# Two AV runs of two head pairs, even fill and late sums in an attention-plus-MoE kernel

## The chip, the cores and the metric

The kernel runs on one core of one Trainium2 chip. The metric is device time in microseconds (us) of one execution. Smaller is better.

## The reference

What is computed, in short. B = 8 batches, H = 8 heads, S = 576 tokens, D = 64:

```python
scores = q @ k.T / sqrt(D)
cum = cumsum(log(clip(f, 1e-4, 1)))              # along the tokens
scores = where(causal, -1e9, scores + cum[:, None] - cum[None, :])
attn = softmax(scores)
x = attn @ v                                     # heads side by side: [4608, 512]
h = x @ w_in                                     # [4608, 2048]
g = 0.5 * h * (1 + erf(h / sqrt(2)))
out = g @ w_out                                  # [4608, 512]
```

The decay is folded into the values: V and a column of ones are multiplied by a weight per key (L253), and the sum of that column divides the result (L318).

## The kernel before, in words

The work goes batch by batch. Each batch has two stages on TensorE (PE): its attention, then GEMM1 (L370), which multiplies the transposed attention output xT of the batch by w_in, 16 blocks of four matmuls, each followed by a gelu on ScalarE (ACT). GEMM2 of a batch isn't a stage of its own: it is the fill of the attention one batch later. The tails of 64 tokens of all batches are put together and go through both GEMMs at the end.

The order on every engine is the order in which the code is written (a manual schedule); nothing moves an instruction. An engine takes its instructions in that order. GEMM2 is a generator, and `take(fill, n)` (L521) writes its next n steps at that point. The lists FILL and FILL_2 (L617, L618) say how many steps follow each score tile.

**Scores.** A pair i holds two heads, on 64 rows of the array each. `scores(b, i, t)` (L270) writes four tiles per pair; a tile takes both heads. Its matmuls use 64 rows, two side by side. ACT takes the exp of each tile (L299) and GpSimd (POOL) clears the entries above the diagonal (L301). The pool `s` has two buffers of two PSUM banks, so a score tile needs the exp of the tile two before it. I write S(i,t) and exp(i,t).

**AV.** `attend` (L313) makes 15 matmuls of 128 rows for one head into a buffer `o`; `normalize` (L318) takes the reciprocal (L333) and multiplies (L334) on VectorE (DVE). Pool `o` has two buffers of one bank, and pool `m` as well. `av(i)` (L627) does both heads of a pair, after S(i+1,1). AV of the last pair comes after all scores.

**Transposes of x.** `x_dma` (L358) lets a DMA on SP's queue do it; `to_xT` (L346) does it on PE, with a copy on DVE. In the batches from 3 on, pairs 0 to 2 go by DMA and pair 3 by PE. In batch 2, pair 2 goes by PE too.

**Fill.** `gemm2_rows(c, plan)` (L446) takes four blocks (ts) of 128 tokens, 16 steps of K = 128 each. A step "n" is one matmul of 128 rows into the first bank. A step "r" is two row-tiled matmuls of 64 rows, one into each of two banks, so an r block needs two banks and a sum at its end: a copy of the second bank (L474), an add of the first (L476), the store (L480). A plan gives each block its pool and its steps (PLAN at L431). Batch 2 has its own fill (L516): half of two blocks of batch 0 (L485, whole matmuls in `m`), two blocks of batch 0 (PLAN_0), then four of batch 1 (PLAN_1).

Batches 0 and 1 have their own functions, which the change leaves alone. A buffer of a pool is given out again when the last reader of what it held is done; of two, the one first free.

Of the kernel before, what the change touches and what calls it, by code (L numbers as in the profile page):

```python
# [1 line left out]

# [6 lines left out]
FP32 = mybir.dt.float32  # L9
BF16 = mybir.dt.bfloat16  # L10
Act = mybir.ActivationFunctionType
Alu = mybir.AluOpType
PSUM = bass.MemoryType.PSUM

P = 128
S = 576
D = 64
H = 8
HP = 4
NBLK = 5  # L20
# [32 lines left out]
def kernel(  # L53
# [10 lines left out]
    nc = tc.nc  # L64
# [5 lines left out]
    n_ff = d_ff // P  # L70
# [17 lines left out]
    s_psum = ctx.enter_context(tc.tile_pool(name="s_psum", bufs=2, space=PSUM))  # L88
    o_psum = ctx.enter_context(tc.tile_pool(name="o_psum", bufs=2, space=PSUM))
    m_psum = ctx.enter_context(tc.tile_pool(name="m_psum", bufs=2, space=PSUM))  # L90
# [46 lines left out]
    for t, op, fill in (  # L137
# [7 lines left out]
            fill=fill,  # L145
# [164 lines left out]

    o_of, x_of, xT_of = {}, {}, {}

    def attend(b, i, h, ms):  # L313
        if (b, i, h) not in o_of:
            o_of[b, i, h] = o_psum.tile([P, NBLK, D + 1], FP32, tag="o", name="o")
        o = o_of[b, i, h]
        for m in ms:
            for n in range(m + 1):  # L318
                t, c = where(n, m)
                nc.tensor.matmul(  # L320
                    o[:, m, :],
                    e_of[b, i, t][:, h, c : c + P],
                    vw_of[b][:, 2 * i + h, n, :],
                    start=(n == 0),
                    stop=(n == m),
                )

    def normalize(b, i, h):
        if (b, i) not in x_of:
            x_of[b, i] = x_pool.tile([P, NBLK, 2, D], BF16, tag="x", name="x")  # L330
        o = o_of[b, i, h]
        r = x_pool.tile([P, NBLK], FP32, tag="r", name="r")
        nc.vector.reciprocal(r, o[:, :, D])  # L333
        nc.vector.tensor_tensor(  # L334
            x_of[b, i][:, :, h, :],
            o[:, :, 0:D],
            r.unsqueeze(2).to_broadcast([P, NBLK, D]),
            Alu.mult,
        )
# [6 lines left out]
    def to_xT(b, i, copy, pool=m_psum, tag="m", ps=None):  # L346
        if ps is None:
            shape = [P, 2, 1024] if pool is s_psum else [P, XC]
            ps = pool.tile(shape, BF16, tag=tag, name="ps_x")
            if pool is s_psum:  # L350
                ps = ps[:, 0, 0:XC]
        for m in range(NBLK):
            nc.tensor.transpose(  # L353
                ps[:, m * P : (m + 1) * P], x_of[b, i][:, m, :, :], ident_bf
            )
        copy(xT(b)[:, i, :], ps)  # L356

    def x_dma(b, i):  # L358
        nc.sync.dma_start_transpose(
            xT(b)[:, i, :].rearrange("d (m p) -> d m p", p=P),  # L360
            x_of[b, i].rearrange("p m h d -> p (m h d)"),
        )
# [31 lines left out]
    def gemm2(c):  # L394
# [34 lines left out]


    PLAN = [  # L431
        (0, "o", 16 * "r"),
        (1, "m", 6 * "r" + "n" + 8 * "r" + "n"),
        (2, "m", 9 * "r" + "n" + 6 * "r"),
        (3, "s", 7 * "r" + 9 * "n"),
    ]

    PLAN_0 = [(2, "o", 16 * "r"), (3, "m", 14 * "r" + 2 * "n")]
    PLAN_1 = [
        (0, "m", 14 * "r" + 2 * "n"),  # L440
        (1, "m", 14 * "r" + 2 * "n"),
        (2, "m", 14 * "r" + 2 * "n"),
        (3, "s", 8 * "r" + 8 * "n"),
    ]

    def gemm2_rows(c, plan):  # L446

        for ts, held, steps in plan:
            if held == "s":
                both = s_psum.tile([P, 2, d_model], FP32, tag="s", name="ps2")
                banks = [both[:, 0], both[:, 1]]
            else:
                pool = {"o": o_psum, "m": m_psum}[held]
                banks = [
                    pool.tile([P, d_model], FP32, tag=held, name="ps2")
                    for _ in range(2)
                ]  # L460
            ot = o_pool.tile([P, d_model], FP32, tag="ot", name="ot")
            for kt, step in enumerate(steps):
                last = kt == steps.rindex("r")
                for r in range(2 if step == "r" else 1):
                    rows = slice(r * D, (r + 1) * D) if step == "r" else slice(0, P)
                    nc.tensor.matmul(  # L466
                        banks[r],
                        g_of[c][kt][rows, ts * P : (ts + 1) * P],
                        w_out_sb[rows, kt, :],
                        start=kt == (steps.index("r") if r else 0),  # L470
                        stop=last if r else kt == n_ff - 1,
                    )
                if kt == n_ff - 1 if held == "s" else last:
                    nc.vector.tensor_copy(ot, banks[1])  # L474
                if kt == n_ff - 1:
                    nc.vector.tensor_tensor(ot, ot, banks[0], Alu.add)  # L476
                    store(c, ts, ot)
                yield

    def store(c, ts, ot):  # L480
        nc.sync.dma_start(out[c * S + ts * P : c * S + (ts + 1) * P, :], ot)
# [39 lines left out]
    def take(gen, n):  # L521
        for _ in range(n):
            if next(gen, "end") == "end":
                return
# [89 lines left out]

    FILL = [[7, 6, 3, 3], [1, 3, 3, 2], [1, 3, 3, 3], [1, 3, 3, 3], [8]]  # L617
    FILL_2 = [[8, 8, 8, 8], [8, 8, 4, 4], [4, 4, 4, 4], [4, 4, 4, 4], [8]]  # L618
    FILL_1 = [[0, 0, 0, 0], [0, 0, 0, 0], [2, 2, 2, 2], [2, 2, 2, 2]]

    def attention(b):


        fill = gemm2_third() if b == 2 else gemm2_rows(b - 1, PLAN)
        counts = FILL_2 if b == 2 else FILL

        def av(i):  # L627
            for h in range(2):
                attend(b, i, h, (0, 1, 2, 3, 4))
                normalize(b, i, h)  # L630

        for i in range(HP):
            for t in range(4):
                scores(b, i, t)
                take(fill, counts[i][t])
                if i and t == 1:
                    av(i - 1)
                    if i < HP - 1 or b > 2:
                        x_dma(b, i - 1)
                if t == 1 and i == 0:  # L640
                    load_v(b + 1)
                if b > 2 and t == 0 and i < 2:
                    transpose_dma(b + 1, 4 * i, 4 * i + 4)
                if b == 2 and t == 1 and i == 1:
                    transpose_dma(3, 0, 4)
                    transpose_dma(3, 4, 8)
        take(fill, counts[HP][0])
        if b == 2:
            to_xT(b, HP - 2, nc.vector.tensor_copy, s_psum, "s")
        av(HP - 1)  # L650
        take(fill, 6)
        to_xT(b, HP - 1, nc.vector.tensor_copy, o_psum, "o")
        x_tail(b)
        take(fill, 999)
# [43 lines left out]
    for b in range(B):  # L698
# [8 lines left out]
        for ffb in range(0 if b > 1 else 4, n_ff):  # L707
# [11 lines left out]
            elif b + 1 < B:  # L719
                first, gap = (5, 3) if b == 1 else (0, 4)  # L720
                at, late = divmod(ffb - first, gap)
# [40 lines left out]
```

The softmax here doesn't subtract the row's maximum and nothing guards it: scores larger than these inputs give would overflow.

## Time and profile before

| what | us |
|---|---|
| median of 3 runs (345.62 to 345.96) | 345.62 |
| span of the profiled execution (first to last instruction) | 343.4 |
| PE busy | 328.6 |
| ACT busy | 212.3 |
| DVE busy | 187.0 |
| POOL busy | 124.2 |
| attention of batch 2, to GEMM1 | 33.0 |
| attention of each batch from 3 on, to GEMM1 | 21.8 |
| GEMM1 of each of these batches | 13.9 |

The page gives the span of the profiled execution and no other time of it. The span leaves out what lies before the first instruction and after the last one, some 2.2 us against the median of the runs. Busy times overlap: the engines work side by side, and the shares don't add up to the span. A line of the timeline gives the start and the length in us, the engine, the line of the code, the operation, what it writes and reads, the rows and columns of the array, the shape, and how many instructions are put together. A matmul's length holds its way through the array: the next one starts before it ends, so the cost of one is read from start to start. In brackets stands the time for which the engine was idle, and what ended it.

### The profile page before, as it was taken

The page shows a single profiled execution, that of the slowest core. Times are in us where ns is not written, and L with a number is a line of the kernel's source. Part 1 is how long each engine was busy: PE and PEld are TensorE (multiplying, and loading weights), DVE is VectorE, ACT ScalarE, POOL GpSimd, SP SyncE. Part 2 cuts the span into 40 slices and gives each one's busy share as a digit, 9 for nine tenths or more (in the row PEclk, how much of TensorE's full clock was granted, in tenths as well). Part 3 has the DMA queues.
Part 4 walks back from the last instruction along what each step waited for, and adds up shares of the span by engine and source line. Part 5 has one row for each costly group of instructions (what it writes and reads, how often), then busy time and mean ns, then how long its engine had stood idle before and what let it go on. Part 6 is the DMA issues. An engine that isn't in the chain of part 4 may idle for free.

```text
span 343.4 us, 7895 instructions
## 1 busy us (share of the span) xinstructions
PE 328.6 (96%) x3182; PEld 174.7 (51%) x3227; DVE 187.0 (54%) x424; ACT 212.3 (62%) x296; POOL 124.2 (36%) x256
## 2 busy tenths in 40 slices
PE   7799999999999999999999999999999999999995
PEld 3574555445554456545654565446544654444443
DVE  5660355933467935796479646974597542020011
ACT  5986786773644787368746874687468755504600
POOL 8390672228328034543445243714261430000000
PEclk9999999999999999999999999999999999999999
DMA  8999999989993999578945896499900230011013
GB/s 117 178 176 194 201 166 153 170 158 148 237 184 102 139 192 188 82 101 165 211 121 73 141 212 139 71 160 198 169 31 2 65 88 31 2 61 61 0 38 87
DMA packets 99924, 43.03 MB, mean 125 GB/s; under 512 B 78704, under 2 KB 95344, under 8 KB 99888
## 3 DMA queue, kind: packets, MB, share of 16 engines
q1 hardware_dynamic: 82592, 28.37, 41.4%
q0 software_dynamic: 16896, 13.63, 27.2%
q8 instruction: 25, 0.41, 0.5%
q10 hardware_dynamic: 400, 0.52, 0.4%
q14 instruction: 11, 0.09, 0.1%
HBM read 36.85 MB, written 9.44 MB: 135 GB/s over the span
## 4 chain that ended last, share of the span: by engine, by line
PE 89%; issue 2%; POOL 2%; DVE 2%; ACT 2%; DMA 2%; POOLq 0%; ACTq 0%; DVEq 0%
PE ps L375 36%; PE ps L466 25%; PE o L320 9%; PE ps L408 8%; PE s L289 7%; PE ps L501 2%; ACT e L299 2%; DMA k<-in_k_dram 2%; PE ps_x L353 1%; DVE x L334 1%; POOL q L107 1%; PE ps_f L206 1%; POOL k L107 1%; DVE r L333 0%; DVE xT L356 0%
## 5 line engine op out<-in xcount | busy, mean ns | idle before, releaser
L392 ACT ACTIVATE g<-ps 128x512 bf16<-128x512 f32 x144 | 85.3, 597 | 81.1 <-PE ps L375 81.1
L299 ACT ACTIVATE e<-s 128x896 bf16<-128x896 f32 (+2 forms) x128 | 101.2, 836 | 28.5 <-PE s L289 26.8
L375 PE MATMUL ps<-xT,w_in_sb 128*128 128x512 bf16 x497 | 111.4, 379 | 0.8
L466 PE MATMUL ps<-w_out_sb,g 64*128 64x512 bf16 (+1 forms) x731 | 103.0, 376 | 0.8 <-issue 0.8
L375 PEld LDWEIGHTS <-w_in_sb 128*128 128x128 bf16 x576 | 56.0, 98 | 67.5 <-issue 1.8
L301 POOL TENSOR_SCALAR_AFFINE_SELECT e<-e 128x256 bf16<-128x256 bf16 (+1 forms) x135 | 49.2, 383 | 98.9 <-ACT e L299 98.6
L466 PEld LDWEIGHTS <-g 64*128 64x128 bf16 (+1 forms) x756 | 41.5, 94 | 40.4 <-issue 11.9
L244 DVE COPY qT<-tq 64x288 bf16<-64x288 bf16 x96 | 48.7, 507 | 1.4
L289 PE MATMUL s<-qT,kT 64*128 64x320 bf16 (+4 forms) x384 | 45.8, 276 | 3.6 <-ACT e L299 2.7
L260 POOL TENSOR_TENSOR vw<-v_sb,wT 128x640 bf16<-128x640 f32 x31 | 39.6, 1278 | 23.5 <-DMA v_sb<-in_v_dram 23.3
L320 PE MATMUL o<-vw,e 128*128 128x65 bf16 x960 | 36.8, 194 | 3.5 <-issue 2.4
L474 DVE COPY ot<-ps 128x512 f32<-128x512 f32 x26 | 17.9, 689 | 37.1 <-PE ps L466 35.2
L320 PEld LDWEIGHTS <-e 128*128 128x128 bf16 x960 | 34.8, 98 | 5.3 <-PE ps_x L353 0.3
L244 DVE COPY kT<-tk 64x288 bf16<-64x288 bf16 x96 | 33.0, 343 | 1.6
L334 DVE TENSOR_TENSOR x<-o,r 128x320 bf16<-128x320 f32 x64 | 31.4, 491 | 2.4 <-DVE r L333 0.2
L417 DVE COPY ot<-ps 128x512 f32<-128x512 f32 (+2 forms) x9 | 5.7, 632 | 48.8 <-PE ps L408 31.9
L289 PEld LDWEIGHTS <-kT 64*128 64x128 bf16 x384 | 19.5, 94 | 23.2 <-issue 9.7
L408 PE MATMUL ps<-w_out_sb,g 128*128 128x512 bf16 (+2 forms) x142 | 27.9, 355 | 0.1
L333 DVE RECIPROCAL r<-o 128x5 f32<-128x5 f32 x64 | 12.1, 189 | 27.6 <-PE o L320 27.5
L408 PEld LDWEIGHTS <-g 128*128 128x128 bf16 x144 | 13.5, 98 | 14.5
L476 DVE TENSOR_TENSOR ot<-ot,ps 128x512 f32<-128x512 f32 x26 | 17.9, 687 | 1.5
L365 POOL COPY tails<-xT 128x256 bf16<-128x256 bf16 x8 | 3.2, 399 | 31.3 <-DVE xT L356 31.3
(64 smaller groups left out, 158.1 us busy)
## 6 DMA issues: line engine op xcount, KB each, us to landing
out_dram<-ot SPq DMA_DIRECT2D x32, 256.0 KB, 2.3
v_sb<-in_v_dram SPq DMA_DIRECT2D x24, 256.0 KB, 5.3
q<-in_q_dram POOLq DMA_DIRECT2D x6, 576.0 KB, 6.1
k<-in_k_dram POOLq DMA_DIRECT2D x6, 576.0 KB, 8.2
v_sb<-in_v_dram SPq DMA_DIRECT2D x22, 128.0 KB, 5.1
w_in_sb<-in_moe_w_in_dram POOLq DMA_DIRECT2D x4, 512.0 KB, 6.7
w_out_sb<-in_moe_w_out_dram POOLq DMA_DIRECT2D x4, 512.0 KB, 8.4
q<-in_q_dram POOLq DMA_DIRECT2D x4, 144.0 KB, 4.6
```

The source lines that it names most:

```text
L244: nc.vector.tensor_copy(rows[:, odd], src[odd * D : (odd + 1) * D, 2 * i + h].rearrange("d j p -> d p j"),)
L260: eng.tensor_tensor(vw_of[b][:, hs, :, 0:D], v_sb[:, hs, :, :], w.unsqueeze(3).to_broadcast([P, 2, NBLK, D]), Alu.mult,)
L289: nc.tensor.matmul(to, *ab, start=half < 0, stop=half == 1 or not masked)
L299: nc.scalar.activation(et[:, :, z:c], st[:, :, z:c], Act.Exp, scale=scale)
L301: nc.gpsimd.affine_select(out=et[:, :, c0 + z : c0 + P], in_=et[:, :, c0 + z : c0 + P], compare_op=Alu.is_ge, fill=0.0, base=z, pattern=[[ ...
L320: nc.tensor.matmul(o[:, m, :], e_of[b, i, t][:, h, c : c + P], vw_of[b][:, 2 * i + h, n, :], start=(n == 0), stop=(n == m),)
L334: nc.vector.tensor_tensor(x_of[b, i][:, :, h, :], o[:, :, 0:D], r.unsqueeze(2).to_broadcast([P, NBLK, D]), Alu.mult,)
L375: nc.tensor.matmul(ps, w_in_sb[:, kt, ffb * P : (ffb + 1) * P], src[:, kt, 0:TC], start=(kt == 0), stop=(kt == n_dm - 1),)
L392: nc.scalar.activation(g_of[c][ffb], ps, Act.Gelu)
L408: nc.tensor.matmul(pss[ts][:, c0:c1], g_of[c][kt][:, ts * P : (ts + 1) * P], w_out_sb[:, kt, c0:c1], start=(kt == 0), stop=(kt == n_ff - 1),)
L466: nc.tensor.matmul(banks[r], g_of[c][kt][rows, ts * P : (ts + 1) * P], w_out_sb[rows, kt, :], start=kt == (steps.index("r") if r else 0), ...
L474: nc.vector.tensor_copy(ot, banks[1])
```

## The change

It touches the attention of batches 2 to 7 and its fill.

- AV of pairs 0 and 1 moves to one place, after S(2,1); AV of pairs 2 and 3 comes after all scores. One step of fill stands after each head of pair 0, one and three after those of pair 2, one after the first of pair 3. The DMA transposes of pairs 0 and 1 move along, and that of pair 2 comes after its AV at the end.
- The last two AV pairs of batch 2 write to pool `m`.
- The steps after each score tile change (FILL, FILL_2), and so do the plans: in PLAN, block 0 is in `m` and block 1 in `o`, blocks 0 and 1 have r alone, block 2 has two n after five r, block 3 is n alone.
- The copy of the second bank of block 2 goes to ACT. Its add and store are put off until after the last AV (`put_off`). A block with no r has a copy in place of a sum.
- In batch 2, the PE transpose of pair 2 moves from ahead of the last AV to behind it, and uses pool `o`.

```diff
--- before.py
+++ after.py
@@ -1,4 +1,5 @@
 from contextlib import ExitStack
+from functools import partial
 
 import concourse.bass as bass
 import concourse.tile as tile
@@ -310,9 +311,9 @@
 
     o_of, x_of, xT_of = {}, {}, {}
 
-    def attend(b, i, h, ms):
+    def attend(b, i, h, ms, pool=o_psum, tag="o"):
         if (b, i, h) not in o_of:
-            o_of[b, i, h] = o_psum.tile([P, NBLK, D + 1], FP32, tag="o", name="o")
+            o_of[b, i, h] = pool.tile([P, NBLK, D + 1], FP32, tag=tag, name="o")
         o = o_of[b, i, h]
         for m in ms:
             for n in range(m + 1):
@@ -429,19 +430,20 @@
 
 
     PLAN = [
+        (0, "m", 16 * "r"),
+        (1, "o", 16 * "r"),
+        (2, "m", 5 * "r" + 2 * "n" + 9 * "r"),
+        (3, "s", 16 * "n"),
+    ]
+
+    PLAN_0 = [(2, "o", 16 * "r"), (3, "m", 10 * "r" + 2 * "n" + 4 * "r")]
+    PLAN_1 = [
         (0, "o", 16 * "r"),
-        (1, "m", 6 * "r" + "n" + 8 * "r" + "n"),
-        (2, "m", 9 * "r" + "n" + 6 * "r"),
-        (3, "s", 7 * "r" + 9 * "n"),
+        (1, "m", 16 * "r"),
+        (2, "o", 16 * "r"),
+        (3, "s", 16 * "n"),
     ]
-
-    PLAN_0 = [(2, "o", 16 * "r"), (3, "m", 14 * "r" + 2 * "n")]
-    PLAN_1 = [
-        (0, "m", 14 * "r" + 2 * "n"),
-        (1, "m", 14 * "r" + 2 * "n"),
-        (2, "m", 14 * "r" + 2 * "n"),
-        (3, "s", 8 * "r" + 8 * "n"),
-    ]
+    put_off = []
 
     def gemm2_rows(c, plan):
 
@@ -459,8 +461,9 @@
                     for _ in range(2)
                 ]
             ot = o_pool.tile([P, d_model], FP32, tag="ot", name="ot")
+            late = len(plan) == 4 and ts == 2
             for kt, step in enumerate(steps):
-                last = kt == steps.rindex("r")
+                last = kt == steps.rfind("r")
                 for r in range(2 if step == "r" else 1):
                     rows = slice(r * D, (r + 1) * D) if step == "r" else slice(0, P)
                     nc.tensor.matmul(
@@ -470,12 +473,19 @@
                         start=kt == (steps.index("r") if r else 0),
                         stop=last if r else kt == n_ff - 1,
                     )
-                if kt == n_ff - 1 if held == "s" else last:
-                    nc.vector.tensor_copy(ot, banks[1])
+                if last:
+                    (nc.scalar.copy if late else nc.vector.tensor_copy)(ot, banks[1])
                 if kt == n_ff - 1:
-                    nc.vector.tensor_tensor(ot, ot, banks[0], Alu.add)
-                    store(c, ts, ot)
+                    out_of = partial(rows_out, c, ts, ot, banks[0], "r" in steps)
+                    put_off.append(out_of) if late else out_of()
                 yield
+
+    def rows_out(c, ts, ot, bank, both):
+        if both:
+            nc.vector.tensor_tensor(ot, ot, bank, Alu.add)
+        else:
+            nc.vector.tensor_copy(ot, bank)
+        store(c, ts, ot)
 
     def store(c, ts, ot):
         nc.sync.dma_start(out[c * S + ts * P : c * S + (ts + 1) * P, :], ot)
@@ -614,8 +624,8 @@
 
 
 
-    FILL = [[7, 6, 3, 3], [1, 3, 3, 2], [1, 3, 3, 3], [1, 3, 3, 3], [8]]
-    FILL_2 = [[8, 8, 8, 8], [8, 8, 4, 4], [4, 4, 4, 4], [4, 4, 4, 4], [8]]
+    FILL = [[7, 6, 3, 3], [3, 3, 3, 3], [3, 3, 0, 1], [2, 2, 2, 2]]
+    FILL_2 = [[8, 8, 3, 3], [3, 3, 3, 3], [4, 4, 4, 8], [10, 10, 10, 10]]
     FILL_1 = [[0, 0, 0, 0], [0, 0, 0, 0], [2, 2, 2, 2], [2, 2, 2, 2]]
 
     def attention(b):
@@ -624,19 +634,24 @@
         fill = gemm2_third() if b == 2 else gemm2_rows(b - 1, PLAN)
         counts = FILL_2 if b == 2 else FILL
 
-        def av(i):
-            for h in range(2):
-                attend(b, i, h, (0, 1, 2, 3, 4))
-                normalize(b, i, h)
+        last = (m_psum, "m") if b == 2 else (o_psum, "o")
+
+        def av(i, h, n=0):
+            attend(b, i, h, (0, 1, 2, 3, 4), *(last if i > 1 else ()))
+            normalize(b, i, h)
+            take(fill, n)
 
         for i in range(HP):
             for t in range(4):
                 scores(b, i, t)
                 take(fill, counts[i][t])
-                if i and t == 1:
-                    av(i - 1)
-                    if i < HP - 1 or b > 2:
-                        x_dma(b, i - 1)
+                if (i, t) == (2, 1):
+                    av(0, 0, 1)
+                    av(0, 1, 1)
+                    x_dma(b, 0)
+                    av(1, 0)
+                    av(1, 1)
+                    x_dma(b, 1)
                 if t == 1 and i == 0:
                     load_v(b + 1)
                 if b > 2 and t == 0 and i < 2:
@@ -644,11 +659,16 @@
                 if b == 2 and t == 1 and i == 1:
                     transpose_dma(3, 0, 4)
                     transpose_dma(3, 4, 8)
-        take(fill, counts[HP][0])
+        av(HP - 2, 0, 1)
+        av(HP - 2, 1, 3)
+        if b > 2:
+            x_dma(b, HP - 2)
+        av(HP - 1, 0, 1)
+        av(HP - 1, 1)
+        put_off.pop()()
         if b == 2:
-            to_xT(b, HP - 2, nc.vector.tensor_copy, s_psum, "s")
-        av(HP - 1)
-        take(fill, 6)
+            to_xT(b, HP - 2, nc.vector.tensor_copy, o_psum, "o")
+        take(fill, 5)
         to_xT(b, HP - 1, nc.vector.tensor_copy, o_psum, "o")
         x_tail(b)
         take(fill, 999)
```

## The prediction

> **What bounds the kernel now.** I read the busy shares first, then the chain of waits, then TensorE's timeline for one batch, then ScalarE's and VectorE's for the same stretch. From the page:
>
> ```profile
> PE 328.6 (96%) x3182; PEld 174.7 (51%) x3227; DVE 187.0 (54%) x424; ACT 212.3 (62%) x296; POOL 124.2 (36%) x256
> PE 89%; issue 2%; POOL 2%; DVE 2%; ACT 2%; DMA 2%; POOLq 0%; ACTq 0%; DVEq 0%
> ```
>
> TensorE (PE) is busy for 96% of the span and carries 89% of the chain that ended last. So a microsecond in which TensorE waits is a microsecond of time, and nothing else matters until it makes TensorE wait. The timeline of TensorE in the attention of batch 4 (start, length, engine, line, count):
>
> ```profile
> 154.77 0.38 PE L375 MATMUL ps<-xT,w_in_sb 128*128 128x512 bf16 x1
> 155.08 0.36 PE L289 MATMUL s<-qT,kT 64*128 64x256 bf16 x4
> 155.28 1.68 PE L466 MATMUL ps<-w_out_sb,g 64*128 64x512 bf16 x14
> ...
> 160.45 0.60 PE L466 MATMUL ps<-w_out_sb,g 64*128 64x512 bf16 x4
> 161.21 1.11 PE L320 MATMUL o<-vw,e 128*128 128x65 bf16 x30 [0.16 <-issue]
> 162.25 0.36 PE L289 MATMUL s<-qT,kT 64*128 64x448 bf16 x2
> 162.45 0.81 PE L466 MATMUL ps<-w_out_sb,g 64*128 64x512 bf16 x6
> 163.10 0.30 PE L289 MATMUL s<-qT,kT 64*128 64x320 bf16 x2
> 163.24 0.59 PE L466 MATMUL ps<-w_out_sb,g 64*128 64x512 bf16 x4
> 163.69 0.37 PE L289 MATMUL s<-qT,kT 64*128 64x256 bf16 x4
> 163.88 0.40 PE L466 MATMUL ps<-w_out_sb,g 64*128 64x512 bf16 x2
> 164.28 0.34 PE L289 MATMUL s<-qT,kT 64*128 64x64 bf16 x4
> ```
>
> Three prices are in it. (1) A step of 512 columns, whole ("n") or as a row-tiled pair ("r"), takes 0.2155 us: seven r from 155.28 to the next scores at 156.79. (2) Mode switches. The last whole matmul of GEMM1 starts at 154.77 and the 64-row scores at 155.08: 0.31, where 0.216 is the matmul, so 0.096 for 128 to 64 rows. From 160.45 to the AV run at 161.21 stand two r and one n (the record of the n is missing): 0.76 - 0.647 leaves 0.11 for 64 to 128. (3) A wait: the tile at 164.28 comes 0.40 after the one r before it instead of 0.2155. That r was all the fill there was, and the tile needs the buffer of the score tile two before it, which ScalarE had not yet read.
>
> Scores cost 0.19, 0.16, 0.19, 0.14 for the four tiles of a pair; an AV run of one head 0.48. Attention takes 21.76 us in each of batches 3 to 7 (155.08 to GEMM1 at 176.85), 33.0 in batch 2 (72.50 to 105.50). ScalarE in the same stretch:
>
> ```profile
> 155.19 0.60 ACT L392 ACTIVATE g<-ps 128x512 bf16<-128x512 f32 x1 [0.27 <-PE ps L375]
> 155.80 1.28 ACT L299 ACT_TABLE_LOAD   x1
> 157.10 4.88 ACT L299 ACTIVATE e<-s 128x896 bf16<-128x896 f32 x6
> 162.72 3.07 ACT L299 ACTIVATE e<-s 128x896 bf16<-128x896 f32 x4 [0.74 <-PE s L289]
> ```
>
> The last gelu of GEMM1 ends at 155.79, which is 0.70 after the attention's first score matmul started. An exp starts 0.47 after its 448-column scores, takes 0.92 (0.81, 0.70 for the narrower tiles) and the next two-tiles-later scores follow 0.05 after its end: scores 162.25, tile two later at 163.69, 1.44 in all. VectorE's normalization of the two heads:
>
> ```profile
> 161.88 0.19 DVE L333 RECIPROCAL r<-o 128x5 f32<-128x5 f32 x1 [1.17 <-PE o L320]
> 162.11 0.49 DVE L334 TENSOR_TENSOR x<-o,r 128x320 bf16<-128x320 f32 x1
> 162.52 0.18 DVE L333 RECIPROCAL r<-o 128x5 f32<-128x5 f32 x1
> 162.74 0.49 DVE L334 TENSOR_TENSOR x<-o,r 128x320 bf16<-128x320 f32 x1
> ```
>
> The first head's last matmul starts at 161.65; its PSUM buffer is free at 162.60, plus 0.05 to reach TensorE: 1.00 in all.
>
> **What the Trainium skill says.** "TensorEngine Tiling (Array Packing)", Key Properties: changing the tiling mode drains TensorE. The trace agrees and prices it at 0.10 to 0.11 us each way. The same page, Gotcha 1 (PSUM Pressure): row tiles write to different banks. The trace's r steps do, and that is why an r block needs two free banks before its first pair. "TensorE: Matmul & The Clock Gate", Part 3 (The mechanism): matmuls start and end strictly in program order. Here the r after a waiting tile never ran ahead of it. So everything behind a waiting matmul waits too.
>
> **The change part by part.** Per batch, for batches 3 to 7.
>
> *Switches.* Before, the order has four passages from 128 to 64 rows (start, and after three AV runs) and four back; the new order has two and two. Two pairs of 0.20: -0.40. The fill n between AV runs is in AV's own mode (0.033 from an AV to an n in the trace), so it adds none. Exchanging 6 r for n costs nothing: both take 0.2155.
>
> *Old waits.* The wait at 164.28 (0.18) and another of 0.18 around 168.4, both behind single-r fills in batch 4's timeline: -0.37. The fills there become 3.
>
> *First block in "m".* Block 0 of the r steps moves from the o buffers, free at that point, to the two m buffers, which GEMM1 used last. The second bank is that of the last gelu. It is free at 0.70 + 0.05 = 0.75; the r wants it at 0.20. Queued behind it is all of TensorE: +0.55. Nothing hides it: S(0,0) is issued, and the next instructions are these very r.
>
> *Two pairs of AV in a row.* Four runs share two o buffers. The third run needs the first's normalization: run start + 0.45 + 1.00 = 1.45, where TensorE arrives at 0.48 + 0.22 + 0.48 + 0.22 = 1.39: +0.06. The fourth needs the second's, whose multiply ends at 2.09, plus 0.05: 2.14; TensorE arrives at 1.93: +0.21. Together +0.27. Entering the run: block 1 now holds o; its last r is five r and two score tiles before it, 1.56 before AV, and the copy needs 0.42 + 0.69, its sum 0.72 more. The first run takes the buffer that the copy frees (1.16), the second, 0.70 later, that of the sum: no wait.
>
> *The tail of scores.* After the AV runs six tiles remain with fills 0, 1, 2, 2, 2, 2. Count from the start of S(2,2). S(3,0) needs exp(2,2): not before 1.43; TensorE arrives at 0.19 + 0.14 + 0.22 = 0.54: wait 0.89. S(3,1): 1.43 + 0.19 + 0.43 = 2.05, exp(2,3) is done at 2.03: none. S(3,2): arrives at 2.64, exp(3,0) runs from 1.92 to 2.84, plus 0.05: 2.89, wait 0.25. S(3,3): arrives at 3.51, exp(3,1) starts 0.81 after the one before and takes 0.81: 3.59, wait 0.07. Together +1.20. ScalarE sat idle during the AV run, and no fill can be done ahead of a waiting tile. AV(2,0) then starts at 4.26.
>
> *Late sums.* The copy of block 2's second bank goes to ScalarE (0.58, from L510's ScalarE copy), behind exp(3,3), about 5.4; its first reader is GEMM1 at 9.9. The add goes behind the last normalization and ends at 8.8. Before that stands the transposing matmul at 8.3, which needs the normalization alone. Cost nothing; cover 1.1 us or more.
>
> *DMAs on SP's queue.* Pairs 0 and 1 are transposed later but 9 us before use. Pair 2's x is normalized at 6.36, issued at 6.4; such transfers landed in 2.6 to 3.9 (median 2.8 in the DMA table): 9.2, at most 10.3. GEMM1 reads it with its third matmul at 9.9 + 0.43 = 10.34. Cost nothing, cover 1.1, none at the slowest. The store of block 1 now precedes the transposes and waits for less than they do; stores and V loads have no reader in this stage. POOL's masks have 0.5 or more to spare.
>
> Sum: -0.40 - 0.37 + 0.55 + 0.27 + 1.20 = +1.25. Adding the new order up from 0 instead (10.36 to the first AV, 13.08 to S(2,2), 9.91 more) gives 22.99, against 21.76: +1.23. Five batches: +6.1.
>
> Batch 2: the old order changes mode at eight places down and eight up (its last block mixes r and n around the transposes), the new at four: -0.80. Old wait before the transpose of pair 3 goes, -0.23. New: AV buffers +0.27; the second transpose waits for the late add, +0.22. Its first r block is in o, as before, and its tail has fills of 8 to 10, over 1.7 us per tile against an exp of 0.92: no tail wait. Sum -0.54; added up from 0, 32.5 against 33.0: -0.5.
>
> In all +6.1 - 0.5 = +5.6 us. The profiled span of 343.4 becomes 349.0; about 2.2 us lie between span and the median of 345.62, unchanged: 351.2.
>
> Bounds: the tail between 0.9 (only the first wait) and 1.4; the gelu wait between 0 (if the allocation differs) and 0.6; AV buffers 0 to 0.5; the direct step from r to AV, which the trace of before lacks, is taken like r to n, 0.11, at most 0.3; never below nothing, since the array must empty. The transfer of pair 2: 0 to 0.6.
>
> **Rivals.** A measurement of this kernel can tell about 0.2%, 0.7 us, from no change.
> - *Pair 2's transfer lands late.* At 4.5 us, what the tq transposes take in the DMA table, it lands at 10.9: 0.58 more, five times: 354.1. Against: the queue is then free, and its like took 2.6.
> - *The gelu wait is covered*, as if the r block began with a free bank: -2.75: 348.5. Against: the order builds r on the buffer of the last gelu.
> - *Only the score tail is covered*: 1.25 - 1.20 = 0.05 a batch, 345.4, no change.
> - *Faster: the mode switches decide.* If neither gelu, AV buffers nor exps hold TensorE, each batch gains 0.77 and batch 2 0.5: 341.3. It decides once the new waits of a batch sum to less than 0.77; for that the tail's first wait would have to vanish, with an exp path of 0.54 where 1.44 is measured.
>
> **How the numbers follow.** My forecast 0.80, late transfer 0.08, gelu covered 0.05, tail covered 0.02, faster 0.05. The likeliest's own range is 349.8 to 352.6 (0.25 a batch either way); the range reaches to 348.5 for the gelu case and 353.2 for part of the transfer's. Faster 0.05, same 0.02, slower 0.93.
>
> **What would show it.** In batch 4: first r's second row half 0.55 behind its first; idle before S(3,0) of some 0.5 to 0.9 on ScalarE's exp (a matmul's tail hides part); 0.2 before the fourth AV run on VectorE; attention at 23.0. In batch 2: 32.5. Wrong if S(3,0) starts within 0.6 of S(2,2), or GEMM1 waits on a DMA.

## The result, and the profile after

The changed kernel takes 354.03 us (median of 5 runs, 352.82 to 356.78), the one before 345.62 (5 runs, 345.02 to 345.96). The ratio is 1.0248 (95% interval 1.0209 to 1.0288): slower, as forecast, but 2.8 us above the forecast of 351.2 and 0.8 outside its range. The profiled execution of the changed kernel took 356.78, the longest of the five: in batch 0, whose code is unchanged, TensorE ran at half its clock for 6.8 us (15.0 to 21.9), and that stage took 19.7 us instead of 17.0. Nothing below is read from that stretch.

The page after, the two lines that were shown of before:

```profile
PE 336.1 (95%) x3162; PEld 180.5 (51%) x3195; DVE 182.6 (51%) x412; ACT 214.2 (60%) x302; POOL 124.8 (35%) x256
PE 69%; SPq 8%; DMA 8%; ACT 5%; POOL 4%; issue 3%; DVE 1%; POOLq 0%; ACTq 0%; DVEq 0%
```

TensorE is as busy as before, but its share of the chain that ended last fell from 89% to 69%. ScalarE, POOL, SP's queue and the DMAs took that share: the chain now runs through other engines more often. The share is no price: 20% of the span would be 71 us, and the loss is 8. Where it lies, the stages tell (start to start of TensorE's first matmul):

| stage | before | after | forecast |
|---|---|---|---|
| attention of batches 3 to 7, each | 21.76 | 22.99 to 23.00 | 22.99 |
| GEMM1 of batches 3 to 6, each | 13.91 | 13.91 | 13.91 |
| attention of batch 2 | 33.00 | 33.88 | 32.5 |
| a wait inside GEMM1 of batch 7 | none | 1.16 | none |

Five times 1.23, 0.88 and 1.16 are 8.2 us, where the medians differ by 8.4. The last two terms are those of one execution and vary, as the experiments show, so that the two totals lie so close is in part chance. (In the two profiled executions the spans differ by 11.7: these 8.2, 2.7 from the clock in batch 0, and 0.7 behind the start of the last matmul, where the final store came in after 4.67 instead of 3.97. In the ten other profiles of this study it took 3.99 to 4.68. What lies outside the span is 1.7 us in the changed kernel, not the 2.2 that the forecast kept: 0.5 less.)

**Batches 3 to 7.** TensorE's timeline of batch 4 after (start, length, engine, line, operation, count, idle time and what ended it):

```profile
160.12 0.38 PE L469 MATMUL ps<-w_out_sb,g 64*128 64x512 bf16 x1
160.67 1.67 PE L469 MATMUL ps<-w_out_sb,g 64*128 64x512 bf16 x13 [0.17 <-ACT g L393]
...
171.45 0.38 PE L469 MATMUL ps<-w_out_sb,g 128*128 128x512 bf16 x1
171.83 1.24 PE L321 MATMUL o<-vw,e 128*128 128x65 bf16 x30
173.00 0.50 PE L290 MATMUL s<-qT,kT 64*128 64x448 bf16 x4
...
174.44 0.37 PE L290 MATMUL s<-qT,kT 64*128 64x256 bf16 x4 [0.72 <-ACT e L300]
...
175.22 0.61 PE L469 MATMUL ps<-w_out_sb,g 64*128 64x512 bf16 x4
175.89 0.37 PE L290 MATMUL s<-qT,kT 64*128 64x448 bf16 x2
...
177.27 0.65 PE L321 MATMUL o<-vw,e 128*128 128x65 bf16 x15
```

Read starts against starts. The second half of the first r (160.67) comes 0.55 behind its first half (160.12), on the last gelu. The bracket says only 0.17, since the first half's modelled length of 0.38 covers the rest of the gap. The first AV run starts 10.36 after the first scores (159.92 to 170.28). S(3,0), at 174.44, comes 1.44 behind S(2,2), on an exp; S(3,2), at 175.89, comes 0.67 behind the two r that begin at 175.22, where 0.43 would do. ScalarE in the same batch:

```profile
160.02 0.60 ACT L393 ACTIVATE g<-ps 128x512 bf16<-128x512 f32 x1 [0.27 <-PE ps L376]
...
173.47 4.48 ACT L300 ACTIVATE e<-s 128x896 bf16<-128x896 f32 x6 [2.85 <-PE s L290]
```

The gelu ends at 160.62, and TensorE goes on 0.05 later. ScalarE stands idle for 2.85 us during the AV runs, then takes six exps back to back in 4.48 us: that is the tail, in which three score tiles come late on ScalarE's exps. VectorE's multiply of the first head (171.19, 0.49 long) ends at 171.68; the third AV run starts at 171.83.

**Batch 2.** TensorE's longer waits in the attention of batch 2 (in total, times, longest); before, this view had only five waits for issue:

```profile
PE ps_x L354 <- ACT ot L477: 0.4, 1, 0.4
PE o L321 <- POOL e L302: 0.3, 1, 0.3
PE ps_x L354 <- DVE ot L485: 0.2, 1, 0.2
```

The timeline behind the second of them, with the line of before ahead of those of after:

```profile
82.29 2.68 POOL L301 TENSOR_SCALAR_AFFINE_SELECT e<-e 128x256 bf16<-128x256 bf16 x8
...
85.61 4.38 POOL L302 TENSOR_SCALAR_AFFINE_SELECT e<-e 128x256 bf16<-128x256 bf16 x13
...
87.03 1.54 PE L321 MATMUL o<-vw,e 128*128 128x65 bf16 x28 [0.26 <-POOL e L302]
```

POOL took V's weighing (L261, 84.24 to 85.52), which waits for V to land, and then 13 masks back to back. AV reads the masked exps, and from its start at 86.54 it follows POOL mask by mask: the second run starts 1.40 after the first instead of 0.70. Before, POOL did the same in this stage, 0.6 earlier in it: the masks ran back to back from 9.8 us after the stage's start. But the first AV run began 11.9 after it and now begins 11.3 after it. The timeline behind the first of them:

```profile
100.95 0.88 SPq L491 DMA_DIRECT2D out_dram<-ot  x1
...
105.19 0.59 ACT L477 COPY ot<-ps 128x512 f32<-128x512 f32 x1 [4.16 <-DMA out_dram<-ot]
...
105.82 0.44 PE L354 MATMUL ps_x<-ident_bf,x 128*128 128x128 bf16 x5 [0.36 <-ACT ot L477]
```

The copy on ScalarE writes an ot, of which there are four. Its buffer still belonged to a store. That store stood on SP's queue behind four transposes of q and k (94.23 to 100.86), was issued at 100.95 and landed at 105.09; the copy starts 0.10 later, and the transposing matmul, which needs the bank that the copy frees, 0.05 after the copy ends. It comes 0.5 after the last AV run should have let it start. Behind the third wait stands VectorE:

```profile
105.77 0.49 DVE L335 TENSOR_TENSOR x<-o,r 128x320 bf16<-128x320 f32 x1 [0.76 <-DMA xT<-x]
```

This multiply for pair 3 overwrites the x of pair 0, since there are three buffers of x. The transfer of pair 0 still read it: it stood on the same queue, behind the four transposes and the store, was issued at 102.02 and landed at 105.68. The late add comes after the multiplies, and the second transposing matmul after the add.

**Batch 7.** GEMM1 waits for pair 2's transfer:

```profile
295.22 2.10 PE L376 MATMUL ps<-xT,w_in_sb 128*128 128x512 bf16 x8 [1.00 <-DMA xT<-x]
```

The third matmul of GEMM1 comes 1.38 after the second (293.84), not 0.216: 1.16 lost. The transfer was issued at 290.11 and landed at 295.18, after 5.07; the same transfer took 2.58 in batches 4 and 5. The bytes on the DMA engines from 289 to 296, in slices of 0.175 us, and the queues in that stretch:

```profile
GB/s 0 0 0 0 0 0 0 0 0 0 0 0 94 140 208 200 152 76 0 0 1 7 10 9 9 113 314 252 347 375 199 0 12 23 35 0 199 386 374 410
...
q14 instruction: 1, 0.01, 1.5%
q8 instruction: 1, 0.02, 1.3%
```

The transfer begins at 291.1, stops at 292.2, and for 1.2 us hardly anything moves (0 to 10 GB/s). In that time two packets are under way that fetch instructions: one of 16 KB on q8 (291.26, 1.41 us) and one of 8 KB on q14 (292.12, 1.69 us). The same view of batch 5's transfer (issued 216.30, landed 218.88) runs through at 138 to 225 GB/s between its first and last slices, with no hole and no fetch.

### The profile page after: what moved, and what is told of

Read it like the earlier page. It is cut to its first block, busy times and chain, and to the rows that moved or that the text cites. A ratio compares the mean times of both kernels' runs of the same rounds, so it can differ in the third digit from the quotient of the medians.

```text
span 355.1 us, 7844 instructions
## 1 busy us (share of the span) xinstructions
PE 336.1 (95%) x3162; PEld 180.5 (51%) x3195; DVE 182.6 (51%) x412; ACT 214.2 (60%) x302; POOL 124.8 (35%) x256
## 3 DMA queue, kind: packets, MB, share of 16 engines
q0 software_dynamic: 16896, 13.63, 26.4%
## 4 chain that ended last, share of the span: by engine, by line
PE 69%; SPq 8%; DMA 8%; ACT 5%; POOL 4%; issue 3%; DVE 1%; POOLq 0%; ACTq 0%; DVEq 0%
PE ps L376 31%; PE ps L469 18%; PE ps L409 8%; PE o L321 7%; SPq L120 5%; PE s L290 4%; ACT e L300 4%; DMA k<-in_k_dram 4%; SPq L231 3%; DMA xT<-x 2%; DMA v_sb<-in_v_dram 2%; POOL vw L261 1%; POOL q L108 1%; ACT g L393 1%; POOL k L108 1%
## 5 line engine op out<-in xcount | busy, mean ns | idle before, releaser
L300 ACT ACTIVATE e<-s 128x896 bf16<-128x896 f32 (+2 forms) x128 | 100.1, 836 | 36.0 <-PE s L290 33.6
L469 PE MATMUL ps<-w_out_sb,g 64*128 64x512 bf16 (+1 forms) x711 | 109.8, 376 | 1.2 <-ACT g L393 0.9
L469 PEld LDWEIGHTS <-g 64*128 64x128 bf16 (+1 forms) x724 | 47.4, 95 | 29.8 <-issue 2.7
L290 PE MATMUL s<-qT,kT 64*128 64x320 bf16 (+4 forms) x384 | 53.2, 282 | 6.8 <-ACT e L300 5.5
L245 DVE COPY qT<-tq 64x288 bf16<-64x288 bf16 x96 | 49.6, 516 | 1.5
L261 POOL TENSOR_TENSOR vw<-v_sb,wT 128x640 bf16<-128x640 f32 x31 | 39.9, 1288 | 22.2 <-DMA v_sb<-in_v_dram 22.1
L321 PEld LDWEIGHTS <-e 128*128 128x128 bf16 x960 | 36.2, 99 | 13.9 <-issue 4.4
L321 PE MATMUL o<-vw,e 128*128 128x65 bf16 x960 | 41.7, 195 | 1.0 <-POOL e L302 0.4
L290 PEld LDWEIGHTS <-kT 64*128 64x128 bf16 x384 | 23.7, 95 | 27.6 <-issue 14.9
L477 DVE COPY ot<-ps 128x512 f32<-128x512 f32 x14 | 9.7, 692 | 38.8 <-PE ps L469 38.8
L376 PE MATMUL ps<-tails,w_in_sb 128*128 128x512 bf16 x63 | 14.3, 378 | 0.1
```

Of the source, the lines that this page charges most:

```text
L245: nc.vector.tensor_copy(rows[:, odd], src[odd * D : (odd + 1) * D, 2 * i + h].rearrange("d j p -> d p j"),)
L261: eng.tensor_tensor(vw_of[b][:, hs, :, 0:D], v_sb[:, hs, :, :], w.unsqueeze(3).to_broadcast([P, 2, NBLK, D]), Alu.mult,)
L290: nc.tensor.matmul(to, *ab, start=half < 0, stop=half == 1 or not masked)
L300: nc.scalar.activation(et[:, :, z:c], st[:, :, z:c], Act.Exp, scale=scale)
L321: nc.tensor.matmul(o[:, m, :], e_of[b, i, t][:, h, c : c + P], vw_of[b][:, 2 * i + h, n, :], start=(n == 0), stop=(n == m),)
L376: nc.tensor.matmul(ps, w_in_sb[:, kt, ffb * P : (ffb + 1) * P], src[:, kt, 0:TC], start=(kt == 0), stop=(kt == n_dm - 1),)
```

## The experiments

My theory has three parts. (1) Batches 3 to 7 lose what the forecast added up: 0.55 on the last gelu, 0.27 on AV's buffers, 1.20 in the tail of scores, less 0.77 for switches and old waits. (2) Batch 2 loses its gain to two queues, POOL's and SP's. (3) GEMM1 of batch 7 waits because instruction fetches fall on the transfer. The rivals: the loss of a batch comes from the longer AV stretch as such and goes with no single wait; the waits of batch 2 are only where a fixed amount of work shows up; pair 2's transfer is late because it is issued late. Stage times below are those of each run's profile. The first kernel is the changed one once more, in other surroundings.

**The changed kernel again.**

> The changed kernel once more, as the measure for the others. Theory: attention of batches 3 to 7 takes 22.99 us each, that of batch 2 33.9, and the span is about 352.4 where TensorE keeps its full clock (in the first profile 6.8 us at half clock in batch 0 added 2.7). Whether GEMM1 of batch 7 waits 1.0 us for the transfer of pair 2 again is open. If the wait is set by where an instruction fetch falls in the program, it comes back in the same place; if it is chance, it is in another batch or absent. Time 352.5 to 355.

Measured: 353.41 us (353.13 to 353.70; ratio 1.021, 1.0176 to 1.0243). Attention 22.99 to 23.00 in each of the five batches; batch 2 33.35; GEMM1 of batch 7 waits again, 0.70 longer than its step, and the transfer (4.61) again has a fetch of 16 KB (288.50) and one of 8 KB (289.35) on it. So the batch term and the place of the late transfer repeat. Batch 2 and the size of the late transfer vary: in the eight profiles in which the code of batch 2 is that of the changed kernel, the stage took 32.99 to 35.10.

**Three whole matmuls ahead of the first scores.** Block 0 starts with three n, taken ahead of S(0,0), so that the first r finds both banks free.

```diff
-        (0, "m", 16 * "r"),
+        (0, "m", 3 * "n" + 13 * "r"),
-    FILL = [[7, 6, 3, 3], ...
+    FILL = [[4, 6, 3, 3], ...
         for i in range(HP):
+        if b > 2:
+            take(fill, 3)
```

> Block 0 starts with three whole steps n, written ahead of the first score tile, so that the second m bank is asked for only after the last gelu has read it. Theory (the first row-tiled pair waits 0.55 us for that gelu, with all of TensorE behind it): attention of batches 3 to 7 goes from 22.99 to 22.44, the time by 5 x 0.55 = 2.7 us, to about 351.3. Rival (the wait is hidden, and the loss of these batches is all in the score tail): 22.99 stays, and the time too.

Measured: 352.66 us (350.90 to 354.42; ratio 1.0189, 1.0140 to 1.0239). Attention with its three n: 36.59 from GEMM1 to GEMM1, against 36.91: -0.32 a batch, not -0.55. The time says less, since batch 2, which the edit leaves alone, took 35.03 in this profile. ScalarE's timeline, and then TensorE's, of batch 4:

```profile
159.69 1.28 ACT L300 ACT_TABLE_LOAD   x1 [0.42 <-PE s L290]
```

```profile
160.45 1.46 PE L469 MATMUL ps<-w_out_sb,g 64*128 64x512 bf16 x12
161.95 0.36 PE L290 MATMUL s<-qT,kT 64*128 64x448 bf16 x2
```

The wait on the gelu is gone. A new one is there: the load of exp's table now waits for the first scores, since it belongs to the first exp, so ScalarE is idle for 0.42 that it had spent loading. S(0,2), at 161.95, comes 1.50 after its six r began, which take 1.29: 0.21 of the 0.55 is given back.

**The same, with the table loaded early.** A one-element exp on ScalarE ahead of the first scores brings the table in. Its output is read by nothing.

```diff
             take(fill, 3)
+            nc.scalar.activation(warm[0:1, 1:2], warm[0:1, 0:1], Act.Exp)
```

> As the kernel with three n ahead of the first scores, and a one-element exp on ScalarE right after them (its output is not used), so that the load of the exp table doesn't stand behind the wait for the first scores. In the run without it the table load began 0.42 us later than it could, S(0,2) waited 0.2 for exp(0,0), and attention with GEMM1 fell by 0.32 and not by 0.55. Theory: with the early load the sum of attention and GEMM1 falls by 0.55 to 36.36. Rival (the gelu wait is worth only 0.32 and the rest is hidden by ScalarE's pace in any case): it stays at 36.59.

Measured: 349.78 us (349.61 to 352.90; ratio 1.0130, 1.0088 to 1.0172). GEMM1 to GEMM1 36.36: -0.55, the whole of the term. ScalarE:

```profile
160.33 1.28 ACT L646 ACT_TABLE_LOAD   x1
...
161.73 4.77 ACT L300 ACTIVATE e<-s 128x896 bf16<-128x896 f32 x6
```

The load follows the last gelu, which ends at 160.31, at once.

**AV two tiles later.** AV of pairs 0 and 1 goes behind S(2,3), and the fill is spread so that more of it stands after the AV runs.

```diff
-    FILL = [[7, 6, 3, 3], [3, 3, 3, 3], [3, 3, 0, 1], [2, 2, 2, 2]]
+    FILL = [[5, 4, 3, 3], [3, 3, 3, 2], [3, 3, 2, 3], [3, 2, 2, 2]]
-                if (i, t) == (2, 1):
+                if (i, t) == (2, 1 if b == 2 else 3):
```

> From batch 3 on the first AV run stands after S(2,3) in place of S(2,1), and the 37 steps ahead of it are spread 5 4 3 3, 3 3 3 2, 3 3 2 3, with 3 2 2 2 after it: two score tiles more are with ScalarE while TensorE does AV. Same instructions, same number of mode switches. Theory (the tail of scores waits 1.20 us for exps because ScalarE idles through the AV run): the tail waits 0.11, attention takes 22.06 in place of 22.99, time down by 4.7 to about 349.4. Rival (the loss comes with the two-pair AV run itself, by its buffers and its switches): the loss stays, 22.7 or more.

Measured: 349.74 us (347.45 to 351.61; ratio 1.0106, 1.0070 to 1.0143). Attention 22.06 in four batches, to the hundredth what was expected, and 22.71 in batch 5. There the transfer of pair 0 took 4.79, with a late multiply of VectorE behind it (0.85 of waiting for the transfer, which still read the x that the multiply overwrites) and a late transposing matmul behind that (0.5). Batch 2, unchanged, took 35.10. Two lines of the tail in batch 4:

```profile
172.09 0.59 PE L469 MATMUL ps<-w_out_sb,g 64*128 64x512 bf16 x4
172.53 0.36 PE L290 MATMUL s<-qT,kT 64*128 64x448 bf16 x2
```

Two r take 0.43, and S(3,2) comes 0.44 after they began. S(3,0) and S(3,2), late by 0.9 and 0.24 in the changed kernel, wait no more; only S(3,3) still comes 0.08 late (173.23, where its two r began at 172.72). The stretch of AV is as long as before, so the loss isn't that of the AV runs as such. It was the wait for the exps behind them.

**One whole matmul between the AV runs of pair 1.** The third n of block 2 moves there.

```diff
-        (2, "m", 5 * "r" + 2 * "n" + 9 * "r"),
+        (2, "m", 5 * "r" + 3 * "n" + 8 * "r"),
-                    av(1, 0)
+                    av(1, 0, 1 if b > 2 else 0)
```

with one step less after S(3,3).

> One of the last tail steps moves between the third and the fourth AV run, as a whole step n, from batch 3 on. Theory (the fourth run waits 0.21 us for VectorE to normalize the second): the step fills that wait, and since it leaves the last fill of the score tail, where it cost its full 0.2155, attention falls by 0.2 from 22.99 to about 22.79. Rival (that gap is an issue cost or a mode matter): 22.99 stays.

Measured: one run, 352.95 us; attention 22.86, -0.14. The AV stretch of batch 4:

```profile
169.05 0.38 PE L469 MATMUL ps<-w_out_sb,g 128*128 128x512 bf16 x1
169.27 0.63 PE L321 MATMUL o<-vw,e 128*128 128x65 bf16 x15
```

The third run (168.58) comes 0.38 after the n before it (168.20), 0.16 late; the fourth, shown, 0.22 after its own, not late. In the changed kernel the third comes 0.38 after its n as well (171.45, 171.83), and from there to S(2,2) it takes 1.17, where two runs of 0.48 and the passage of 0.10 are 1.06: the fourth was 0.11 late. So the sum of 0.27 was right, but it was split 0.16 and 0.11, not 0.06 and 0.21, and only the second part could be covered here.

**One more pair of switches.** The ninth step of block 1, amid row-tiled work, becomes a whole matmul.

```diff
-        (1, "o", 16 * "r"),
+        (1, "o", 8 * "r" + "n" + 7 * "r"),
```

> One r in the middle of block 1, between score tiles ahead of AV, becomes an n: one more passage to 128 rows and back in each batch from 3 on, all else equal. Theory (a pair of passages costs 0.20, and nothing waits there for ScalarE): attention 23.19 to 23.2 in place of 22.99. Rival (the drain overlaps, and the two pairs that the change saves bring nothing): 22.99.

Measured: one run, 354.47 us; attention 23.20 to 23.21, +0.21. That is the price of a pair of passages by itself; the forecast used 0.20.

**The transposes of batch 3 behind the AV runs.** In batch 2, the transposes of q and k for batch 3 are issued after x's of pair 1, no longer at S(1,1).

```diff
                     x_dma(b, 1)
+                    if b == 2:
+                        transpose_dma(3, 0, 4)
+                        transpose_dma(3, 4, 8)
-                if b == 2 and t == 1 and i == 1:
-                    transpose_dma(3, 0, 4)
-                    transpose_dma(3, 4, 8)
```

> In batch 2 the four transposes of q and k for batch 3 are issued after those of x, as they stood behind a store and the first x before the change. Theory (block 2's copy on ScalarE waits for a store to land, which is queued behind these four): the copy starts at once after its block, about 26.5 after the stage's start in place of 29.3 to 31, the first PE transpose follows the last AV without a wait (0.3 to 0.6 us gone) and batch 2 is shorter by about as much. Rival: the copy is late for ScalarE's own work, nothing changes. The wait at the first AV run, on POOL, stays in any case.

Measured: one run, 354.85 us, of which 1.7 more than before were spent ahead of batch 2, where the edit changes nothing; batch 2 32.94. From the timeline:

```profile
93.25 0.62 SPq L491 DMA_DIRECT2D out_dram<-ot  x1
...
96.73 1.32 SPq L231 DMA_TRANSPOSE tq<-q  x1
...
101.11 0.59 ACT L477 COPY ot<-ps 128x512 f32<-128x512 f32 x1 [1.39 <-PE ps L469]
```

The store goes out ahead of the transposes. The copy waits for TensorE alone and ends 2.3 us ahead of the transposing matmul (103.99), which follows AV's last matmul within 0.03. VectorE's multiply for pair 3 has no wait either. What is left is 0.41 on POOL's masks in the first two AV runs; without it, 32.5, the forecast. The waits on the queue are gone, but the length of the stage alone doesn't show what they cost: the run with other fetch positions, below, leaves batch 2 as it is and took 32.99. There the store landed after 2.74 instead of 4.14, in time for the copy, and 0.48 on masks was all the waiting. The order on the queue makes the store late, and its landing decides what that costs.

**In batch 2, AV two tiles later too.** On top of that edit:

```diff
-    FILL_2 = [[8, 8, 3, 3], [3, 3, 3, 3], [4, 4, 4, 8], [10, 10, 10, 10]]
+    FILL_2 = [[8, 8, 3, 3], [3, 3, 2, 2], [2, 2, 3, 3], [13, 13, 13, 13]]
-                if (i, t) == (2, 1):
+                if (i, t) == (2, 3 if b == 2 else 1):
```

> The same, and in batch 2 the first AV run stands after S(2,3), with fills 8 8 3 3, 3 3 2 2, 2 2 3 3, 13 13 13 13. Theory (the first AV waits for POOL's masks, which are behind the weighting of V, itself behind the landing of V): AV starts 0.3 to 0.5 later and waits that much less; no other change. With V landing as late as in the slowest runs seen, a wait stays. Rival (the wait is on ScalarE's exps): it stays as it is.

Measured: one run, 353.46 us; batch 2 32.99. The second AV run starts 0.70 after the first: no wait on masks. This doesn't show that the later AV run takes the wait away, for V's weighing began 1.59 after the start of the stage here and 2.97 after it in the run before, early enough for AV behind S(2,1) too. And two score tiles now wait for an exp: S(1,2) comes 0.66 after its two r began (80.77, 81.43), which take 0.43, so 0.23 late, and S(2,0), at 82.89, is 0.24 late. The fills of two that I had put there aren't enough to hide an exp. So the edit cost 0.47 on ScalarE, and the stage didn't come under 32.9.

**Other fetch positions.** In batch 0, 64 matmuls of 64 columns whose result is not read shift TensorE's instructions against the time of later stages.

```diff
+        for _ in range(64):
+            nc.tensor.matmul(
+                psx[:, 0:D], warm[:, 0:P], warm[:, 0:D], start=True, stop=True
+            )
```

> 64 matmuls of 64 columns on the zero tile are added in batch 0, where TensorE waits for q and k anyway; they shift every later instruction of TensorE by 128 places [...] and change nothing else. Their output is not read. Theory (the transfer of pair 2 in batch 7 took 5.1 instead of 2.6 because a fetch of TensorE's instructions held one of the DMA engines just then): the fetch moves some 5 us ahead, GEMM1 of batch 7 waits less than 0.3, time down by about 1. Rival (the transfer is late there for its place in the kernel, by stores or by the queue): it takes about 5 again and GEMM1 waits 1.0.

Measured: 353.37 us (353.21 to 353.92; ratio 1.0212, 1.0184 to 1.0241). GEMM1 of batch 7 waits for nothing: its transfer took 3.54, with no 16 KB packet on it and one of 8 KB that took 0.31. Batch 0 took 18.26 instead of 16.70 in the run of the changed kernel beside it, so the time as a whole shows nothing. No 16 KB fetch on the transfer, no wait, and the issue was as late as before: 3.95 ahead of the time at which GEMM1 wants the data, as in all other runs of the changed order. This goes with the third part and against a late issue. The 16 KB fetches come once per some 250 of TensorE's instructions (25 in the profile after, for 6357), and they moved with the shift; the 8 KB fetch stayed 2.0 us behind the issue. One of the 16 KB fetches now fell on pair 2's transfer in batch 5: it took 3.19 there, where the changed kernel had 2.58 and no fetch.

All profiles with the changed kernel or an edit of it together have 54 transfers of pair 2 by DMA in batches 3 to 7. In 27 of them no fetch was under way from 0.9 us after the issue on, when the packets move: they took 2.55 to 2.60. In the other 27 one or two were: they took 2.77 to 5.32, with no overlap between the groups. With one 16 KB fetch it was 2.77 to 3.65, with the 8 KB fetch alone 3.54, and with both 4.37 to 5.32. Both fell on batch 7's in each of these profiles in which a DMA made it, save the shifted one, and in each of these nine GEMM1 waited.

**The edits together.** Three n ahead of the first scores with the table early, AV behind S(2,3) in all batches, the transposes moved, an n between the runs of pair 1, and in batch 7 pair 2 transposed by TensorE instead of a DMA. Block 2 becomes four r, three n, nine r. Besides the lines shown above:

```diff
-    FILL = [[7, 6, 3, 3], [3, 3, 3, 3], [3, 3, 0, 1], [2, 2, 2, 2]]
+    FILL = [[4, 5, 3, 3], [3, 3, 3, 2], [2, 2, 2, 1], [3, 2, 2, 2]]
-        if b > 2:
+        if 2 < b < B - 1:
             x_dma(b, HP - 2)
...
         take(fill, 5)
+        if b == B - 1:
+            to_xT(b, HP - 2, nc.vector.tensor_copy, o_psum, "o")
```

> All together from batch 3 on: three n ahead with the early table load, first AV run after S(2,3), fills 4 5 3 3, 3 3 3 2, 2 2 2 1, 3 2 2 2, a third n between the last two of the four AV runs; in batch 2 the later AV run and the changed queue; in batch 7 pair 2 transposed by TensorE, so that no instruction fetch can hold it up. Theory: attention with GEMM1 35.4 us against 35.67 of the kernel before and 36.9 of the changed one; batch 2 about 32.7; time 344 to 345.5, at or a little below the kernel before. Rival (the waits removed come back elsewhere, ScalarE being the limit of the 12 tiles ahead of AV): 346 to 348.

Measured: 345.79 us (22 runs, 345.08 to 349.98) against 345.75 of the kernel before (27 runs, 345.06 to 349.52): ratio 0.9998, 0.9976 to 1.0020. It makes up the whole loss and wins nothing that can be measured; the 344 to 345.5 that was expected it misses. Batch 2 takes 32.99, GEMM1 has no wait on a DMA, and a batch takes 35.58 from GEMM1 to GEMM1 (before: 35.67), batch 7 with its second transpose on TensorE 0.28 more. The single terms would give 36.91 - 0.55 - 0.94 - 0.14 = 35.28. The missing 0.30 stands in TensorE's timeline of batch 4: S(2,0) starts at 164.43, two r (0.43) having begun at 163.76, and S(0,2) at 158.27, five r (1.08) having begun at 157.09. They are 0.24 and 0.10 late on exps that ran back to back on ScalarE from 157.33: fill given to the later tiles is missing at the early ones.

## Why the prediction was right, and where it was wrong

**Batches 3 to 7: right, to 0.01 us in each.** The sum added up from zero gave 22.99; measured are 22.99 to 23.00. Of its terms:

- Switches, 0.20 a pair: 0.21 by the added pair. The timeline has two passages each way, where it had four.
- First block in "m", +0.55: 0.55 in the timeline, and 0.55 once it was removed with nothing put in its place. That the first removal gave 0.32 shows the cover that the term had: behind the waiting r, ScalarE was loading a table.
- AV's buffers, +0.27: 0.27, but the third run waits longer than I had it (it starts 0.15 after the multiply's end, not 0.05) and the fourth correspondingly less. The sum stands because the fourth run's start is set by VectorE, whenever the third began: 2.15 behind the first run, where 2.14 was forecast.
- Tail of scores: S(3,0) 1.44 behind S(2,2) (forecast 1.43), AV(2,0) at 4.27 (forecast 4.26). Moving the AV runs took the waits away and gave 22.06, as expected from the same prices.
- Late sums: nothing in these batches, as forecast. The copy on ScalarE follows the last exp.

So the direction and 6.15 us of the loss come out of the prices in the profile before.

**Batch 2: wrong.** The failed step is "-0.5" (32.5 against 33.0); it was +0.88, 1.4 off. The work was summed rightly: without the waits named below, 32.5 is left in both profiles of the changed kernel and in the one with the moved transposes. Three sentences on slack carried the step.

- "POOL's masks have 0.5 or more to spare": the wait was 0.70. The first AV run of this stage had moved 0.63 ahead against the masks, and these stand behind V's weighing, which waits for V to land. In the nine profiles with AV at its new place, the wait is the start of the weighing (from the start of the stage) less 2.55 to 2.60: 2.87 gives 0.27, 3.27 gives 0.70, 4.35 gives 1.75, and 2.33 gives none. So V's landing sets it, and with it most of what batch 2 varies by. Before, the weighing began at 2.68, which would cost some 0.1.
- "Stores and V loads have no reader in this stage": the next writer of an ot buffer waits until the store that reads the old content has landed. The store stands behind four transposes on SP's queue, because the AV runs moved later while those transposes stayed at S(1,1). The wait was 0.51, and it was gone when the transposes were moved. In the seven other profiles that left the order alone it was 0.2 to 0.7 in five and nothing in two: in one the store landed after 2.7 instead of 3.9 to 4.8, in the other the masks had held AV back by 1.2 before.
- "Pairs 0 and 1 are transposed later but 9 us before use" looked at GEMM1 alone. VectorE overwrites pair 0's x before that. The second transposing matmul came 0.36 late in all, where 0.22 was forecast. In each profile with more than the forecast there, VectorE's multiply for pair 3 waited for the transfer (0.32 to 0.98); in those without, it did not.

0.70, 0.51 and 0.14 are 1.35 of the 1.4.

**The transfer of pair 2: wrong once in five.** The failed step is "Cost nothing, cover 1.1, none at the slowest". In four batches that held. In batch 7 GEMM1 waited on a DMA, which the prediction had named as a sign of being wrong: the transfer took 5.07, outside the 2.6 to 3.9 that I took as its range. The trace of before had transfers of x at 4.01, 4.11 and 4.88, each with a fetch of 16 KB on it; the range left them out. They did no harm there: the two longest were issued 5.5 and 5.9 us ahead of the matmul that reads them. Here it is 3.95. The rival "pair 2's transfer lands late" gave 354.1, nearly the time measured, but for another reason: it had all five batches late by 0.58, where one was late by 1.16 and batch 2 was 1.4 off. (These two, and 0.7 for the final store less 0.5 outside the span, make about 2.8 us.) A matching total is not a matching mechanism.

**What stays open.** Whether a fetch lay on it tells the longer transfers of pair 2 from the shorter in all 54 cases, and one run moved the fetches and with them the length. Why so little moves for 1.2 us, no run here shows. Why V lands in batch 2 at such different times (its weighing began 1.59 to 4.35 us after the start of the stage) was not tested.

## What to carry to other kernels

Price an edit from start-to-start times in the stage it touches, and count which buffer each new reader needs: five stages were forecast to 0.01 us in this way. A slack is true only of the stage in which it was read; work it out again for each stage that has other work in the same queues, and treat a store or a transfer as the reader of its buffer until it lands. Ask of each wait that is to be removed what ran beneath it: here it was a table load, and the fill that covered one tile was then missing at another.

## What the runs showed of the hardware

- A load of ScalarE's table is done with the first activation that needs it, and waits for that activation's input: 0.42 us of idle time ahead of a load of 1.28 when the scores came later. A one-element exp of 0.20 took the load out of that wait.
- DMA transposes of pair 2 took 2.55 to 2.60 us with no instruction fetch on them, 2.77 to 3.65 with one of 16 KB (0.88 to 1.41 us long), and 4.37 to 5.32 with one of 16 KB and one of 8 KB. The fetches come at set places of the program, so batch 7 was hit by both in nine of the ten profiles in which it transposed pair 2 by DMA.
- A store holds its buffer until it lands. In batch 2, with four transposes ahead of it on the queue, the one that mattered was issued 25.2 to 26.4 us into the stage and landed 2.7 to 4.8 later; with the transposes behind it, it was issued 19.1 into it.
- A passage from 64 rows to 128 and back costs 0.21 us, measured by adding one.
- The clock was halved for 3.4 to 6.8 us in batch 0 of three of the profiled executions, with no change in that code; that stage took 18.2 to 19.9 us there, 16.5 to 17.0 in the eight others with the same code and the full clock.
